# Linear attention and an erf-gated MLP: one-pass products for all units of the second group, and the output product moved ahead of h

## The chip, the cores and the metric

One core of a Trainium2 chip runs the whole kernel. The metric is the device time of the program in microseconds, lower is better. TensorE is called PE in the profile (its weight loads PEld), VectorE DVE, ScalarE ACT, GpSimd POOL and the queue that issues most DMAs SP.

## The reference

```python
# q, k, v: (8, 8, 576, 64), w_in: (512, 2048), w_out: (2048, 512), all float32
kv  = einsum('bhsd,bhse->bhde', k, v)
o   = einsum('bhsd,bhde->bhse', q, kv)
x   = o / sqrt(mean(o * o, axis=-1) + 1e-6) * g_norm      # per head
x   = x.transpose(0, 2, 1, 3).reshape(4608, 512)
h   = x @ w_in                                            # (4608, 2048)
g   = h * erf(log1p(exp(h)))                              # erf of softplus
out = g @ w_out                                           # (4608, 512)
```

## The kernel before

The 4608 tokens are worked in nine groups of 512 columns. Group T holds 512 tokens of batch T; the last group holds the 64 tokens that are left over in each batch. For a group, x lies transposed as xT (four chunks of 128 rows by 512 tokens). The 2048 columns of h are cut into FC = 16 chunks, so a group has 16 units. For each unit the kernel computes h (128 by 512, "hidden"), softplus and erf on ScalarE, the gate `h * s` on VectorE, and the output product of that unit, which adds into four PSUM banks `o_ps`. For groups 0 and 1 (FIRST = 2) a single loop over n = 0 .. 32 goes through the units, n = 16 T + f; for the groups after them a second loop works in batches of four units.

**Two ways to compute a product.** The plain way gives float32 operands to TensorE (L940 for h: four products, which the profile shows as eight instructions; L645 for the output: likewise). The one-pass way (`product`, L589, called by `hidden`) splits both operands. x becomes x_high (rounded, ScalarE, L527), x_low (VectorE, L530) and x_both (VectorE, L533); a weight tile becomes three parts through `w_upper` (one ScalarE operation, L551) and `w_lower` (two VectorE operations, L554 and L557, then a store of the parts to DRAM for the later groups). n_ps takes eight one-pass matmuls (x_high and x_low), m_ps four (x_both). The results are joined by a scaled copy of n_ps on ScalarE (L955) and an add of m_ps on VectorE (L567).

Group 0 uses the plain way throughout. In group 1 the first WHOLE = 2 units (16 and 17) are plain and the others are one-pass. The list `to_cut` says which weight tiles are split in which unit of group 1: in unit f the tile of w_in for unit f + 2, and one of `others` (w_in 0 and 1, then the tiles of w_out); `places_w` adds a third in some units, kept in room that used-up tiles of w_in leave. The parts lie in the pool `w_in_p` with four buffers, which stands where the pool `early` (raw weights, first loads) stood, and is opened when `early` is closed.

**Order.** The order of each engine's instructions is the order in which the program writes them, by hand; engines wait for each other by semaphores. The output product lags: at n, output(n - LAG) with LAG = 5 is computed, in front of it the gate has run at n - 1 (`done = n - LAG + 1`). In group 0 the gate is written ahead of h; in group 1 it is written behind the evacuation:

```python
                nc.scalar.activation(h, n_ps, AF.Copy, scale=SHIFT - 1.0)
                add(h, m_ps)
            if T == FIRST - 1:
                ...
                gates(done)
```

Within one n of group 1 the order before is: pieces of attention at place 3, `w_lower` of tiles cut at n - 1, pieces at place 0 (norm or split), h products, evacuation, gate of unit n - 4, `w_lower` of the third tile, `w_upper` of new tiles, softplus, pieces at place 1 (visit or mean), erf for some units, output(n - 5), and pieces at place 2. The pieces prepare x of the next group: in group 0 that of group 1, in group 1 that of group 2. A "visit" is attention's products on TensorE (L404, L412, L418), a "mean" the sums of squares (L456, L457), followed by Ln, Exp and Square on ScalarE and the norm (L476, L479, L488) with a transpose (L329) on VectorE.

`erf` runs in batches [...] (table loads at L113, L116, L885). `sums` copies the four banks of a finished group out, and `store` sends them to DRAM. Weights arrive as pairs of 32-bit words and are joined to float32 by `w_split` and `w_join` in group 0.

Of the kernel before, what the change touches and what calls it, by code (L numbers as in the profile page):

```python
# [40 lines left out]
FP32R = mybir.dt.float32r  # L41
# [9 lines left out]
BATCH = 4  # L51
LAG = 5
# [1 line left out]


FIRST = 2
WHOLE = 2
SHIFT = 4096.0
SQ = 32
ORDER = """  # L60
# [9 lines left out]
def kernel(  # L70
# [11 lines left out]
    P = 128  # L82
    B, H, S, D = q.shape
    DM, DF = moe_w_in.shape[0], moe_w_in.shape[1] // 2
    J = 4
    G = J * P
    R = S - G
    NP = H // 2
    KC = DM // P
    FC = DF // P  # L90
# [200 lines left out]
    def weights():  # L291

        w_next("split")
        w_next("join")
        w_next("load")
# [229 lines left out]
    def upper(x, high):  # L525

        nc.scalar.activation(high, x, AF.Copy, scale=1.0 + 2.0**-13)  # L527

    def lower_only(x, high, low):
        nc.vector.tensor_tensor(out=low, in0=x, in1=high.bitcast(FP32), op=ALU.subtract)  # L530

    def both_only(high, low, both):
        nc.vector.scalar_tensor_tensor(  # L533
            out=both,
            in0=low.bitcast(FP32),
            scalar=SHIFT,
            in1=high.bitcast(FP32),
            op0=ALU.mult,
            op1=ALU.add,
        )  # L540
# [75 lines left out]
    def w_lower(which, f):  # L616

        t, x, parts = w_new.pop((which, f))
        lower_w(x, *(parts[:, i] for i in range(3)))
        kept = w_kept[which, f] = dram.tile([P, 3, G], FP32, name=f"w_{which}{f}")  # L620
        for i in range(3):
            if t is None:
                nc.sync.dma_start(
                    out=kept[:, i].rearrange("p (c f) -> p c f", c=KC), in_=parts[:, i].bitcast(FP32)
                )
        if t is not None:
            nc.sync.dma_start(out=kept, in_=t.bitcast(FP32))
            if which == "in" and f >= WHOLE:
                w_now[which, f] = [t]

    def hidden(T, f, turns=True):
# [9 lines left out]
    def project(f, g, last):  # L641
        for j in range(J):
            if f == 0:
                o_ps[j] = ps_o.tile([P, DM], FP32, name=f"o_ps{j}", tag=f"o{j}")
            nc.tensor.matmul(  # L645
                o_ps[j],
                lhsT=g[:, j * P : j * P + P],
                rhs=w_out_sb[:, f, :],
                start=(f == 0),
                stop=last,  # L650
            )
# [16 lines left out]
    es = {}  # L668
# [187 lines left out]

    others = [("in", f) for f in range(WHOLE)]
    others += [("out", f) for f in (*range(FC - BATCH, FC), *range(FC - BATCH))]  # L860
    places_w = {3: 0, 5: 1, 6: 0, 8: 1, 9: 2, 10: 0}
    to_cut = {f: [] for f in range(FC)}
    for f in range(FC):
        if f < FC - BATCH:
            to_cut[f] = [others.pop(0), ("in", f + WHOLE)]
        elif f == FC - BATCH:
            to_cut[f] = [("in", FC - 2), ("in", FC - 1)]
        if f in places_w:
            to_cut[f].append((*others.pop(0), places_w[f]))
# [10 lines left out]
    def gates(n):  # L880
        nc.vector.tensor_tensor(out=hs[n], in0=hs[n], in1=ss[n], op=ALU.mult)  # L881

    def erf(units):
        for i in units:
            nc.scalar.activation(ss[i], ss[i], AF.Erf)  # L885

    for n in range(FIRST * FC + 1):
        T, f = divmod(n, FC)
        if n == FC:
            early_room.close()  # L890
            late = ctx.enter_context(tc.tile_pool(name="late", bufs=1))
            x_new = ctx.enter_context(tc.tile_pool(name="x_new", bufs=1))
            acc = ctx.enter_context(tc.tile_pool(name="acc", bufs=1))
            w_in_p = ctx.enter_context(tc.tile_pool(name="w_in_p", bufs=BATCH))
            low = low_room.enter_context(tc.tile_pool(name="low", bufs=1))
            forms = late.tile([P, 3, KC, G], FP32R, name="x_forms0")
            x_forms[FIRST] = [forms[:, i] for i in range(3)]
        if T < FIRST:
            if f == 0:
                steps = pieces_of(T + 1)  # L900

            if due(0 if n == 2 * (BATCH - 1) else 1):
                weights()
            while kept:
                keep_prepared()
            for piece in steps[f][3]:
                piece()
            for key in list(w_new)[:2]:
                w_lower(*key)
            for piece in steps[f][0]:  # L910
                piece()
        while due(0):
            weights()
        done = n - LAG + 1
        if T == 0 and done >= 0:
            gates(done)
        if T == FIRST - 1:
            if f == 0:
                x_high = wide.tile([P, KC, G], FP32R, name="x_high", tag="a")
                x_low = low.tile([P, KC, G], FP32R, name="x_low")  # L920
                for i in range(0, KC, 2):
                    upper(xT[T][:, i : i + 2], x_high[:, i : i + 2])
                for i in range(0, KC, 2):
                    lower_only(xT[T][:, i : i + 2], x_high[:, i : i + 2], x_low[:, i : i + 2])
        if T == FIRST - 1 and f >= WHOLE:
            n_ps, m_ps = hidden(T, f, turns=False)
        elif T < FIRST:

            if n >= AHEAD:
                plain[n] = ps_h.tile([P, G], FP32, name="h_ps", tag="h")  # L930
                blocks = [(n, c) for c in range(KC)]
            elif n == 0:
                for i, (pool, tag) in enumerate(((ps_now[0], "at"), (ps_now[0], "at"), (ps_o, "o0"))):
                    plain[i] = pool.tile([P, G], FP32, name="h_ps", tag=tag)
                blocks = [(i, c) for c in range(2) for i in range(2)]
                blocks += [(2, 0), (2, 1)] + [(i, 2) for i in range(3)] + [(0, KC - 1)]
            else:
                blocks = [(n, KC - 1)]
            for i, c in blocks:
                nc.tensor.matmul(  # L940
                    plain[i],
                    lhsT=w_in_sb[:, i % FC, c],
                    rhs=xT[T][:, c, :],
                    start=(c == 0),
                    stop=(c == KC - 1),
                )
        if T < FIRST:
            if n == whole:
                old_h = acc.tile([P, BATCH, G], FP32, name="h", tag="e")
            h = hs[n] = old_h[:, n - whole] if n >= whole else unit("h_sb")  # L950
            s = ss[n] = unit("s_sb")
            if n in plain:
                nc.scalar.copy(h, plain.pop(n))
            else:
                nc.scalar.activation(h, n_ps, AF.Copy, scale=SHIFT - 1.0)  # L955
                add(h, m_ps)
            if T == FIRST - 1:
                if f == 1:
                    x_both = wide.tile([P, KC, G], FP32R, name="x_both", tag="b")
                    for i in range(0, KC, 2):  # L960
                        both_only(x_high[:, i : i + 2], x_low[:, i : i + 2], x_both[:, i : i + 2])
                    x_forms[T] = x_high, x_low, x_both
                gates(done)
                for key in list(w_new):
                    w_lower(*key)
                for key in to_cut[f]:
                    w_upper(*key)
            if T == FIRST - 1 and f and f % BATCH == 0:
                erf(range(n - BATCH // 2, n))
                softplus_table()  # L970
            nc.scalar.activation(s, h, AF.Softplus)
            for piece in steps[f][1]:
                piece()
            if f % BATCH == BATCH - 1:
                apart = T == FIRST - 1 and f < FC - 1
                erf(range(n - BATCH + 1, n + 1 - (BATCH // 2 if apart else 0)))
                if not apart:
                    softplus_table()
            if T == FIRST - 1:
                load_parts("in", {FC - 3: 2, FC - 2: 1, FC - 1: 1}.get(f, 0))  # L980
        if n >= LAG:
            T2, f2 = divmod(n - LAG, FC)
            last = n - LAG in (FC - 1, whole - 1)
            project(f2, hs[n - LAG], last)
            if last:
                sums(*((acc, "e") if T2 < FIRST - 1 else (wide, "a")))
                if T2 == 0:
                    for j in range(J):
                        store(T2, j, es.pop(j))
        if T < FIRST:  # L990
            for piece in steps[f][2]:
                piece()
            fetch_some(4)
# [49 lines left out]
    for m in range(first_batch, batches + 1):  # L1043
# [10 lines left out]
        def piece():  # L1054
            if todo:
                todo.pop(0)()
# [129 lines left out]
```

## Time and profile before

| what | value |
|---|---|
| median of 3 runs | 907.0 us (906.57 to 907.75) |
| profiled execution | 907.2 us, of which the span is 905.4 us |
| TensorE busy | 897.1 us, 99% |
| VectorE busy | 758.7 us, 84% |
| ScalarE busy | 593.2 us, 66% |
| DMA | 259.89 MB, mean 287 GB/s |
| group 1's products | 125 to 238 us |
| granted TensorE clock | 0.999 |

The page gives for each engine its busy time, and then the chain of work that ended last, followed back from the end. A line of a timeline has the start in us, the length in us, the engine, the line of the kernel, the operation, what it writes and reads, how many instructions are merged, and in brackets how long the engine was idle before it and what ended that. A matmul's end is modelled, and matmuls overlap by pipelining, so the distance between starts says more than the lengths.

### The profile page before, as it was taken

How to read it: one execution, taken by the hardware profiler on the slowest of the kernel's cores; microseconds unless marked ns; L12 is line 12 of the kernel's file. 1: busy time of each engine (PE TensorE's matmuls, PEld its weight loads, DVE VectorE, ACT ScalarE, POOL GpSimd, SP SyncE). 2: the span in 40 equal slices, each digit the busy share in tenths (PEclk: the TensorE clock that was granted, in tenths of full speed). 3: DMA queues.
4: the chain of work that ended last, by engine and by line, in shares of the span. 5: the costliest groups of instructions: out<-in, count | busy, mean ns of one | idle time of the engine just before them, and what ended most of it. 6: DMA issues, size and time to landing. Idle time of an engine off the chain costs nothing.

```text
span 905.4 us, 13399 instructions
## 1 busy us (share of the span) xinstructions
PE 897.1 (99%) x4934; PEld 667.6 (74%) x4934; DVE 758.7 (84%) x1093; ACT 593.2 (66%) x784; POOL 4.7 (1%) x14
## 2 busy tenths in 40 slices
PE   8999999999999999999999999999999999999998
PEld 4444446666688888888888888888888888888886
DVE  5799959997788888888888888888888888887677
ACT  5976677775766666665666666666666766665552
POOL 2000000000000000000000000000000000000000
PEclk9999999999999999999999999999999999999999
DMA  9977308999599988988899879988797788778871
GB/s 290 300 225 222 100 30 289 367 343 354 200 377 375 328 297 262 376 306 300 300 328 364 310 238 327 362 303 305 277 346 274 266 311 311 285 285 314 320 265 48
DMA packets 136930, 259.89 MB, mean 287 GB/s; under 512 B 78817, under 2 KB 87265, under 8 KB 136865
## 3 DMA queue, kind: packets, MB, share of 16 engines
q1 hardware_dynamic: 136128, 258.09, 81.3%
q10 hardware_dynamic: 544, 0.82, 0.3%
q8 instruction: 39, 0.64, 0.3%
q14 instruction: 27, 0.21, 0.1%
q0 software_dynamic: 192, 0.13, 0.0%
HBM read 224.40 MB, written 34.60 MB: 286 GB/s over the span
## 4 chain that ended last, share of the span: by engine, by line
PE 94%; DMA 2%; DVE 2%; ACT 1%; issue 0%; SPq 0%; DVEq 0%
PE n_ps L589 48%; PE m_ps L589 24%; PE o_ps L645 10%; PE h_ps L940 5%; PE at_ps L418 2%; PE at_ps L404 2%; DMA w_out_parts<-w_out 1%; DMA w_raw<-in_moe_w_out_dram 1%; PE at_ps L456 1%; PE at_ps L457 1%; PE warm_ps L792 1%; DVE w_e L267 0%; PE o_ps L712 0%; DVE w_in_sb L274 0%; DVE h L881 0%
## 5 line engine op out<-in xcount | busy, mean ns | idle before, releaser
L589 PE MATMUL n_ps<-w_out_parts,g_forms 128*128 128x512 f32 x928 | 230.5, 390 | 0.1
L589 PE MATMUL n_ps<-x_forms,w_in_parts 128*128 128x512 f32 x896 | 224.3, 392 | 0.0
L589 PEld LDWEIGHTS n_ps<-w_out_parts,g_forms 128*128 128x128 f32 x928 | 172.7, 188 | 36.0 <-DMA w_out_parts<-w_out 0.5
L589 PEld LDWEIGHTS n_ps<-x_forms,w_in_parts 128*128 128x128 f32 x896 | 166.6, 188 | 35.6 <-ACT s_sb L885 0.2
L567 DVE TENSOR_TENSOR h<-m_ps,h 128x512 f32<-128x512 f32 x116 | 78.1, 687 | 63.9 <-PE m_ps L589 61.9
L589 PE MATMUL m_ps<-w_out_parts,g_forms 128*128 128x512 f32 (+1 forms) x468 | 124.2, 388 | 0.0
L589 PE MATMUL m_ps<-x_forms,w_in_parts 128*128 128x512 f32 x448 | 119.7, 389 | 0.0
L1092 ACT ACTIVATE h<-n_ps 128x512 f32<-128x512 f32 x112 | 66.2, 594 | 75.0 <-PE n_ps L589 74.7
L1097 ACT ACTIVATE s<-h 128x512 f32<-128x512 f32 x112 | 68.3, 629 | 70.0 <-DVE h L567 70.0
L645 PE MATMUL o_ps<-w_out_sb,h_sb 128*128 128x512 f32 x224 | 101.5, 596 | 0.2 <-DVE h_sb L881 0.2
L589 PEld LDWEIGHTS m_ps<-w_out_parts,g_forms 128*128 128x128 f32 x468 | 87.4, 188 | 18.4
L589 PEld LDWEIGHTS m_ps<-x_forms,w_in_parts 128*128 128x128 f32 x448 | 84.1, 188 | 17.5
L567 DVE TENSOR_TENSOR e<-m_ps,e 128x512 f32<-128x512 f32 (+1 forms) x117 | 80.3, 687 | 15.4 <-PE m_ps L589 5.6
L645 PEld LDWEIGHTS o_ps<-w_out_sb,h_sb 128*128 128x128 f32 x224 | 41.3, 189 | 45.3 <-issue 43.1
L533 DVE SCALAR_TENSOR_TENSOR g_forms<-g_forms 128x1024 fp32r<-128x1024 f32 x58 | 71.1, 1225 | 2.0
L530 DVE TENSOR_TENSOR g_forms<-h,g_forms 128x1024 fp32r<-128x1024 f32 x58 | 70.5, 1216 | 1.1 <-ACT g_forms L527 1.1
L527 ACT ACTIVATE g_forms<-h 128x1024 fp32r<-128x1024 f32 x58 | 58.4, 1049 | 15.3 <-DVE h L1146 7.9
L562 DVE SCALAR_TENSOR_TENSOR e<-n_ps,e 128x512 f32<-128x512 f32 x88 | 60.2, 684 | 7.3 <-PE n_ps L589 7.3
L940 PE MATMUL h_ps<-xT,w_in_sb 128*128 128x512 f32 x144 | 65.1, 595 | 1.1 <-DVE w_in_sb L274 1.1
L1146 DVE TENSOR_TENSOR h<-h,s 128x1024 f32<-128x1024 f32 x56 | 65.9, 1218 | 0.0
L116 ACT ACT_TABLE_LOAD x44 | 56.5, 1283 | 0.8
L940 PEld LDWEIGHTS h_ps<-xT,w_in_sb 128*128 128x128 f32 x144 | 26.9, 190 | 35.4 <-issue 31.4
(138 smaller groups left out, 999.0 us busy)
## 6 DMA issues: line engine op xcount, KB each, us to landing
w_out_parts<-w_out SPq DMA_DIRECT2D x116, 768.0 KB, 6.8
w_in_parts<-w_in SPq DMA_DIRECT2D x112, 768.0 KB, 6.7
w_in<-w_new SPq DMA_DIRECT2D x16, 768.0 KB, 4.6
k_sb<-in_k_dram SPq DMA_DIRECT2D x32, 288.0 KB, 6.3
v_sb<-in_v_dram SPq DMA_DIRECT2D x31, 288.0 KB, 6.3
w_raw<-in_moe_w_in_dram SPq DMA_DIRECT2D x16, 512.0 KB, 5.6
w_raw<-in_moe_w_out_dram SPq DMA_DIRECT2D x8, 1024.0 KB, 5.1
out_dram<-e SPq DMA_DIRECT2D x32, 256.0 KB, 3.5
```

The costliest lines, as they stand in the source:

```text
L116: nc.scalar.preload_act_table_set("softplus")
L527: nc.scalar.activation(high, x, AF.Copy, scale=1.0 + 2.0**-13)
L530: nc.vector.tensor_tensor(out=low, in0=x, in1=high.bitcast(FP32), op=ALU.subtract)
L533: nc.vector.scalar_tensor_tensor(out=both, in0=low.bitcast(FP32), scalar=SHIFT, in1=high.bitcast(FP32), op0=ALU.mult, op1=ALU.add,)
L562: nc.vector.scalar_tensor_tensor(out=out_, in0=ps, scalar=scale, in1=out_, op0=ALU.mult, op1=ALU.add)
L567: nc.vector.tensor_tensor(out=out_, in0=ps, in1=out_, op=ALU.add)
L589: nc.tensor.matmul(ps[:, cols], lhsT=weights(form, k), rhs=moving(form, k)[:, cols], start=(form == forms[0] and k == 0), stop=(form == fo ...
L645: nc.tensor.matmul(o_ps[j], lhsT=g[:, j * P : j * P + P], rhs=w_out_sb[:, f, :], start=(f == 0), stop=last,)
L940: nc.tensor.matmul(plain[i], lhsT=w_in_sb[:, i % FC, c], rhs=xT[T][:, c, :], start=(c == 0), stop=(c == KC - 1),)
L1092: nc.scalar.activation(h[:, i], n_ps, AF.Copy, scale=SHIFT - 1.0)
L1097: nc.scalar.activation(s[:, i], h[:, i], AF.Softplus)
L1146: nc.vector.tensor_tensor(out=part(h, half), in0=part(h, half), in1=part(s, half), op=ALU.mult)
```

## The change

WHOLE is gone: units 16 and 17 are computed by `hidden` like the others. What they need is made in unit n = 15, the last of group 0. The pool `early` is closed and its successors are opened there (after a loop that joins any weights still left), `w_upper` is called for w_in 0 and 1, and, as `w_lower` follows in the same unit, both tiles are split and stored there; x_high is rounded behind unit 15's softplus and ahead of its erf. x_low and x_both are made at the head of n = 16. `others` loses its first two entries and `places_w` the entries of units 3 and 5 of the group. From n = 16 on, the output product, now the function `output`, is written ahead of the h products of the same n; for n < 16 it stays where it was. The gates stay where they were.

```diff
 FIRST = 2
-WHOLE = 2
...
-            if which == "in" and f >= WHOLE:
+            if which == "in":
                 w_now[which, f] = [t]
...
-    others = [("in", f) for f in range(WHOLE)]
-    others += [("out", f) for f in (*range(FC - BATCH, FC), *range(FC - BATCH))]
-    places_w = {3: 0, 5: 1, 6: 0, 8: 1, 9: 2, 10: 0}
+    others = [("out", f) for f in (*range(FC - BATCH, FC), *range(FC - BATCH))]
+    places_w = {6: 0, 8: 1, 9: 2, 10: 0}
...
-            to_cut[f] = [others.pop(0), ("in", f + WHOLE)]
+            to_cut[f] = [others.pop(0), ("in", f + 2)]
...
+    def output(i):
+        T2, f2 = divmod(i, FC)
+        last = i in (FC - 1, whole - 1)
+        project(f2, hs[i], last)
+        if last:
+            sums(*((acc, "e") if T2 < FIRST - 1 else (wide, "a")))
+            if T2 == 0:
+                for j in range(J):
+                    store(T2, j, es.pop(j))
+
     for n in range(FIRST * FC + 1):
         T, f = divmod(n, FC)
-        if n == FC:
-            early_room.close()
...
         if T < FIRST:
             if f == 0:
                 steps = pieces_of(T + 1)
             if due(0 if n == 2 * (BATCH - 1) else 1):
                 weights()
+            if n == FC - 1:
+                while w_at["join"] < len(w_order):
+                    weights()
+                early_room.close()
...
+                for i in range(2):
+                    w_upper("in", i)
             while kept:
                 keep_prepared()
...
         if T == 0 and done >= 0:
             gates(done)
+        if n == FC:
+            x_low = low.tile([P, KC, G], FP32R, name="x_low")
+            for i in range(0, KC, 2):
+                lower_only(xT[T][:, i : i + 2], x_high[:, i : i + 2], x_low[:, i : i + 2])
+            x_both = wide.tile([P, KC, G], FP32R, name="x_both", tag="b")
+            for i in range(0, KC, 2):
+                both_only(x_high[:, i : i + 2], x_low[:, i : i + 2], x_both[:, i : i + 2])
+            x_forms[T] = x_high, x_low, x_both
+        if n >= FC:
+            output(n - LAG)
         if T == FIRST - 1:
-            if f == 0:
-                x_high = wide.tile([P, KC, G], FP32R, name="x_high", tag="a")
...
-        if T == FIRST - 1 and f >= WHOLE:
             n_ps, m_ps = hidden(T, f, turns=False)
...
             nc.scalar.activation(s, h, AF.Softplus)
             for piece in steps[f][1]:
                 piece()
+            if n == FC - 1:
+                x_high = wide.tile([P, KC, G], FP32R, name="x_high", tag="a")
+                for i in range(0, KC, 2):
+                    upper(xT[1][:, i : i + 2], x_high[:, i : i + 2])
...
-        if n >= LAG:
-            T2, f2 = divmod(n - LAG, FC)
-            last = n - LAG in (FC - 1, whole - 1)
-            project(f2, hs[n - LAG], last)
...
+        if LAG <= n < FC:
+            output(n - LAG)
```

More of the change, by code (lines that the diff above doesn't have):

```diff
@@ L885, in erf @@
             nc.scalar.activation(ss[i], ss[i], AF.Erf)
+    def output(i):
[7 more added lines that the diff above has]
+                    store(T2, j, es.pop(j))
     for n in range(FIRST * FC + 1):
         T, f = divmod(n, FC)
-        if n == FC:
-            early_room.close()
[L891 to L897, printed above, removed]
         if T < FIRST:
@@ L903 @@
                 weights()
+            if n == FC - 1:
+                while w_at["join"] < len(w_order):
+                    weights()
+                early_room.close()
+                late = ctx.enter_context(tc.tile_pool(name="late", bufs=1))
+                x_new = ctx.enter_context(tc.tile_pool(name="x_new", bufs=1))
+                acc = ctx.enter_context(tc.tile_pool(name="acc", bufs=1))
+                w_in_p = ctx.enter_context(tc.tile_pool(name="w_in_p", bufs=BATCH))
+                low = low_room.enter_context(tc.tile_pool(name="low", bufs=1))
+                forms = late.tile([P, 3, KC, G], FP32R, name="x_forms0")
+                x_forms[FIRST] = [forms[:, i] for i in range(3)]
+                for i in range(2):
+                    w_upper("in", i)
             while kept:
@@ L916 @@
             gates(done)
-        if T == FIRST - 1:
-            if f == 0:
-                x_high = wide.tile([P, KC, G], FP32R, name="x_high", tag="a")
[L920 to L924, printed above, removed]
-        if T == FIRST - 1 and f >= WHOLE:
+        if n == FC:
[8 more added lines that the diff above has]
+            output(n - LAG)
+        if T == FIRST - 1:
             n_ps, m_ps = hidden(T, f, turns=False)
@@ L957 @@
             if T == FIRST - 1:
[L958 to L962, printed above, removed]
                 gates(done)
@@ L980 @@
                 load_parts("in", {FC - 3: 2, FC - 2: 1, FC - 1: 1}.get(f, 0))
-        if n >= LAG:
-            T2, f2 = divmod(n - LAG, FC)
-            last = n - LAG in (FC - 1, whole - 1)
-            project(f2, hs[n - LAG], last)
[L985 to L989, printed above, removed]
+        if LAG <= n < FC:
+            output(n - LAG)
         if T < FIRST:
```

## The prediction

> **What bounds the kernel now.** I read the page's busy times and chain, then the table of windows for the second group's stretch, then the timeline by engine there.
>
> ```profile
> PE 897.1 (99%) x4934; PEld 667.6 (74%) x4934; DVE 758.7 (84%) x1093; ACT 593.2 (66%) x784; POOL 4.7 (1%) x14
> ...
> PE 94%; DMA 2%; DVE 2%; ACT 1%; issue 0%; SPq 0%; DVEq 0%
> ```
>
> TensorE is busy for 99% of the span and carries 94% of the chain that ended last: whatever lengthens its queue lengthens the kernel. The second group (units 16 to 31) lies at 125 to 238 us, and inside it TensorE has no hole at all (columns: window, its length, then busy us of PE, PEld, DVE, ACT and POOL):
>
> ```profile
> 135.00:178.00 43.00, 43.00 (x229) 26.31 (x228) 39.14 (x65) 32.51 (x51) 0.00 (x0) 1.00 0.90 324
> ```
>
> The chain in order of time gives the price of a plain h (four products in full fp32, eight instructions) and of an output product: 3.43 us each.
>
> ```profile
> 125.32 3.43 PE h_ps L940 x8
> 128.75 3.43 PE o_ps L645 x8
> 132.18 3.43 PE h_ps L940 x8
> ```
>
> A later unit, on TensorE's timeline, has the one-pass h (n_ps, then m_ps) followed by its output product:
>
> ```profile
> 175.87 1.10 PE L589 MATMUL m_ps<-x_both,w_new 128*128 128x512 f32 x4
> 176.80 3.60 PE L645 MATMUL o_ps<-w_out_sb,h_sb 128*128 128x512 f32 x8
> 179.84 0.79 PE L589 MATMUL n_ps<-x_high,w_new 128*128 128x512 f32 x1
> ...
> 182.11 1.10 PE L589 MATMUL m_ps<-x_both,w_new 128*128 128x512 f32 x4
> 183.04 3.60 PE L645 MATMUL o_ps<-w_out_sb,h_sb 128*128 128x512 f32 x8
> ```
>
> From output to output is 183.04 - 176.80 = 6.24 us; less 3.43, the one-pass h costs 2.81. Now what VectorE does when an h is finished, where it was waiting for it:
>
> ```profile
> 189.55 0.69 DVE L567 TENSOR_TENSOR h_sb<-m_ps,h_sb 128x512 f32<-128x512 f32 x1 [0.67 <-PE m_ps L589]
> 190.16 0.68 DVE L881 TENSOR_TENSOR h_sb<-h_sb,s_sb 128x512 f32<-128x512 f32 x1
> ```
>
> The add of m_ps (unit n), and right behind it the gate (L881) of unit n-4, which the *next* output product reads. Today the whole of hidden(n+1) lies between this gate and its reader, so it costs nothing. Only once does an output product follow without an h between: the last of the group.
>
> ```profile
> 233.65 0.68 DVE L881 TENSOR_TENSOR h_sb<-h_sb,s_sb 128x512 f32<-128x512 f32 x1
> ...
> 234.38 0.30 PEld L645 LDWEIGHTS o_ps<-w_out_sb,h_sb 128*128 128x128 f32 x2 [1.06 <-DVE h_sb L881]
> 234.38 0.70 PE L645 MATMUL o_ps<-w_out_sb,h_sb 128*128 128x512 f32 x1 [0.23 <-DVE h_sb L881]
> ```
>
> There the weight load starts 0.05 us after the gate's end (233.65 + 0.68 = 234.33), and TensorE stands.
>
> [...] No view of this kernel shows a lower clock (1.00 even in the first 10 us, where TensorE idled 1.5 us), so no run here shows a fall.
>
> **The change part by part.**
>
> *Units 16 and 17 in one-pass products.* Removed 2 x 3.43, added 2 x 2.81: -1.24 us, all on TensorE's path. Two more copies with scale and two adds of m_ps (0.60 and 0.69) lie on ScalarE and VectorE beside TensorE's work. The evacuation of both banks has an output product (3.43) over it as before.
>
> *The output product ahead of h, for n >= 16.* The order becomes output(n-5), h(n), output(n-4), h(n+1). Output(n-4) needs gate(n-4), and the code still issues that gate behind the add of unit n, which needs the last product of h(n). So after every h TensorE waits. Take m_ps starting at S (four products). TensorE is free for the next at S + 0.93 (175.87 to 176.80). The add starts at S + 1.20 (188.35 to 189.55), the gate 0.61 later (190.16 - 189.55), it takes 0.68, the load starts 0.05 after, and the unprefetched load costs 0.11 (234.38 to the next h's first product at 237.52 is 3.14, against 179.84 - 176.80 = 3.03). The gap is 1.20 + 0.61 + 0.68 + 0.05 + 0.11 - 0.93 = 1.72 us. It comes after h(16) to h(31), 16 times: 27.5 us.
>
> Part of it is filled. Attention's pieces for group 2 stand between h and the next output: four visits (162.40 to 163.79, 1.39 us) after units 17, 21, 25, 29, and four means (170.08 to 170.55, 0.47) after 18, 22, 26, 30. They ran before too, so 4 x 1.39 + 4 x 0.47 = 7.44 comes off: 20.1 us remain.
>
> VectorE must be at the add on time. A unit now takes 6.24 + 1.72 = 7.96 us. From add to add VectorE needed 8.12 before units 23 and 27 (170.35 to 178.47): 0.15 late each. Before unit 31 it is 8.96 (224.09 to 233.05; the norm waits for ScalarE's root): 1.0 late. Sum 1.3 (0 to 4). The old wait and unprefetched load at 234.38 (0.23 + 0.11) go: -0.3.
>
> *Splits in unit 15.* Two weight splits put two copies (0.52 spacing) on ScalarE, four operations (2.65, spacings at 131.94 to 134.59) on VectorE and two stores of 768 KB on SP. ScalarE reaches them when the last table load of unit 14 ends, at 119.17 + 1.28 = 120.45, and had 1.47 us idle there: free. SP issues nothing from 103.5 to 133.4 and POOL nothing at all, so the stores pass nobody. VectorE is another matter: the diff puts the four operations ahead of this:
>
> ```profile
> 119.19 0.69 DVE L476 SCALAR_TENSOR_TENSOR u<-at_ps,u 128x512 f32<-128x512 f32 x1 [3.61 <-ACT u L470]
> ...
> 121.43 0.78 DVE L329 STREAM_TRANSPOSE qT<-q_sb 128x576 f32<-128x576 f32 x1
> 122.13 0.65 DVE L881 TENSOR_TENSOR h_sb<-h_sb,s_sb 128x512 f32<-128x512 f32 x1
> ```
>
> They start at about 121.1 (first copy's end), so the norm begins at 123.8 rather than 119.2 and gate(11) ends at 123.77 + 2.94 + 0.68 = 127.39 instead of 122.78. It feeds output(11), now the next thing after output(10), whose end is 125.15. TensorE waits until 127.44, plus 0.11: 2.4 us. Nothing in the old trace shows this; bounds are 0 (should the gate come in time) and 4 (should the copies be held too).
>
> *x split.* The two roundings (2.0 us on ScalarE) go ahead of unit 15's erf, the four VectorE operations (4.8) to the head of unit 16. x_high is done at about 127.1 (its second half waits for the norm, 126.0), x_low at 129.8, x_both at 132.1; h(16) starts at 127.55 + 3.4 = 130.9 and wants x_both at 132.8: hidden by output(11), with 0.7 us to spare. The erf of units 12 to 15 ends near 130.6 instead of 126.7; gate(12) asks for it at 134.7: free.
>
> *Rest.* The join loop ahead of the new pools finds nothing left (the last join ends at 115). The third cut of units 19 and 21 is gone from ScalarE (0.52) and VectorE (1.3), both off the path. Sums of group 0 and their four stores come one h earlier, behind the same output(15), with 2.81 us of h over 1.4 us of copies: nothing. At the end h(31) lies behind output(26), leaving output(27) and eight of group 2's products before its sums' banks and gates are wanted; the longest chain I can follow (erf, copies, cut, evacuation of unit 32) has over 3 us left: nothing, 0 to 2.
>
> Sum: -1.2 + 20.1 + 1.3 - 0.3 + 2.4 = **+22.3 us**. The profiled execution took 907.2 (span 905.4 and 1.8 around it), 0.2 above the median of 907.0, so 929.5 against it and **929** against the median. A measurement can tell about 0.2% (1.8 us) from no change.
>
> **The rivals.** *A: the gate is early.* If output(n-4)'s gate ended before h(n) did, the gaps vanish, and so would the stall: 907.0 - 1.2 - 0.3 = 905.5, ahead by 0.17%, with a little luck by more. The mechanism would be slack on VectorE: it waits idle before 189.55. Against it: those 0.67 us are a wait for m_ps itself, and the add stands in front of the gate in one queue. It decides below a gap of 0.2 us: eight units have no piece to fill it, and 8 x 0.2 is the 1.5 us gained. Add and gate alone take 1.29. Chance 3%.
>
> *B: as forecast but without the stall in unit 15 and with lags hidden*: 929 - 2.4 - 1.3 = 925. Some 15%, inside the range.
>
> *C: the gaps slow TensorE's clock.* It would idle 1.72 of 7.96 us, 22%. [...] Against it, [...] a clock of 1.00 at 0 to 10 us in spite of gaps. Chance 4%.
>
> *D: the split does not reach units 16 and 17's products in time*, so that h(16) waits for x_both beyond the 0.7 us: 929 + 3 = 932. Some 10%, inside.
>
> **How the numbers follow.** Forecast with B and D 93%, A 3%, C 4%. The gap at 1.5 or 1.95 instead of 1.72 moves 16 x 0.22 = 3.5 either way; the stall 0 to 4; lags 0 to 4. Low: 929 - 2.4 - 3.5 = 923; high: 929 + 3.5 + 3.5 = 936. Faster by over 0.2%: 1%; within: 2%; slower: 97%.
>
> **What would show it.** In the new profile the output product's weight loads (L645's counterpart) should wait for the gate 16 or 17 times, some 20 to 27 us in all; TensorE busy in the second group should fall to near 85%; output to output should be about 8.0 us with or without a visit between; later stages should keep their lengths. I am wrong if outputs come 6.2 us apart, if the waits name another releaser (x_both, m_ps), or if the clock drops below 1.00.

## The result, and the profile after

| | before | changed |
|---|---|---|
| median, us | 907.35 (906.57 to 907.75) | 930.82 (928.47 to 932.16) |
| ratio to before, 95% interval | | 1.0254 (1.0242 to 1.0267) |
| profiled execution, us (span) | 907.2 (905.4) | 931.17 (929.4) |
| TensorE busy, us | 897.1 | 901.6 |
| granted TensorE clock, mean | 0.999 | 0.995 |

The kernel is 2.5% slower. (907.35 takes in a fourth run of the kernel before; the prediction had three, 907.0.) The page of the changed kernel, busy times and chain by engine:

```profile
PE 901.6 (97%) x4942; PEld 669.8 (72%) x4942; DVE 760.8 (82%) x1095; ACT 593.9 (64%) x784; POOL 4.7 (1%) x14
...
PE 90%; DVE 5%; DMA 2%; ACT 2%; SPq 1%; issue 1%; DVEq 0%; ACTq 0%
```

TensorE's busy time rose by only 4.5 us while the span rose by 24.0: most of the loss is idle time. VectorE's share of the chain went from 2% to 5%. The waits inside the second group (engine and line that waited, for whom, us in total, times, longest), TensorE's rows only:

```profile
PE o_ps L644 <- DVE h_sb L879: 19.6, 17, 2.5
```

There is one kind of wait: the output product waits for the gate, 17 times. The table of windows for the whole stretch (window, length, busy us of PE, PEld, DVE, ACT, POOL, clock, DMA share, GB/s):

```profile
125.00:262.00 137.00, 117.42 (x538) 68.59 (x537) 93.73 (x153) 83.18 (x124) 0.00 (x0) 0.98 0.66 236
262.00:929.00 667.00, 662.74 (x3753) 543.95 (x3751) 566.70 (x786) 421.16 (x540) 0.00 (x0) 1.00 0.85 302
```

TensorE is busy for 86% of the group's stretch and 99% of the rest. Its timeline for the same unit as in the prediction (h of unit 23, then the next output; first an output behind a mean):

```profile
184.37 3.70 PE L644 MATMUL o_ps<-w_out_sb,h_sb 128*128 128x512 f32 x8 [0.98 <-DVE h_sb L879]
192.29 3.70 PE L644 MATMUL o_ps<-w_out_sb,h_sb 128*128 128x512 f32 x8 [1.48 <-DVE h_sb L879]
200.20 3.70 PE L644 MATMUL o_ps<-w_out_sb,h_sb 128*128 128x512 f32 x8 [1.45 <-DVE h_sb L879]
208.10 3.70 PE L644 MATMUL o_ps<-w_out_sb,h_sb 128*128 128x512 f32 x8 [0.16 <-DVE h_sb L879]
```

Outputs now come 7.9 us apart. With nothing between h and output the idle time is 1.45 to 1.48, with a mean 0.98, with a visit 0.16; the distance is the same in all three cases, since the gate, not the piece, ends the gap. (The idle time counts from a matmul's modelled end, the gap in the prediction from when the next could have started, 0.17 earlier, plus 0.11 for the unprefetched load.)

VectorE at units 15 and 16:

```profile
121.07 0.69 DVE L553 SCALAR_TENSOR_TENSOR w_new<-w_new,w_in_sb 128x512 fp32r<-128x512 f32 x1 [5.55 <-ACT w_new L550]
...
123.73 0.68 DVE L475 SCALAR_TENSOR_TENSOR u<-at_ps,u 128x512 f32<-128x512 f32 x1
...
126.67 0.65 DVE L879 TENSOR_TENSOR h_sb<-h_sb,s_sb 128x512 f32<-128x512 f32 x1
```

The weight splits wait 5.55 us for ScalarE's copies, the norm stands behind them, and the gate of unit 11 behind the norm, 4.5 us later than before. TensorE pays for it, and then for something else (outputs 10 and 11, h of unit 16, output 12):

```profile
121.65 3.60 PE L644 MATMUL o_ps<-w_out_sb,h_sb 128*128 128x512 f32 x8
127.37 5.40 PE L644 MATMUL o_ps<-w_out_sb,h_sb 128*128 128x512 f32 x8 [2.13 <-DVE h_sb L879]
132.21 0.80 PE L588 MATMUL n_ps<-x_high,w_new 128*128 128x512 f32 x1
...
134.43 1.09 PE L588 MATMUL m_ps<-x_both,w_new 128*128 128x512 f32 x4
136.97 3.70 PE L644 MATMUL o_ps<-w_out_sb,h_sb 128*128 128x512 f32 x8 [1.45 <-DVE h_sb L879]
140.11 0.80 PE L588 MATMUL n_ps<-x_high,w_new 128*128 128x512 f32 x1
```

The eight instructions of output 12 take 140.11 - 136.97 = 3.14 us from their first start to the next product's start; those of output 11 take 132.21 - 127.37 = 4.84. The windows give the reason (the number behind POOL's is the clock):

```profile
128.00:129.00 1.00, 1.00 (x3) 0.43 (x2) 1.00 (x2) 0.99 (x3) 0.00 (x0) 0.57 0.00 0
129.00:130.00 1.00, 1.00 (x2) 0.33 (x1) 0.97 (x2) 1.00 (x3) 0.00 (x0) 0.50 0.00 0
130.00:131.00 1.00, 1.00 (x2) 0.33 (x1) 1.00 (x2) 0.98 (x3) 0.00 (x0) 0.50 0.00 0
131.00:132.00 1.00, 1.00 (x3) 0.52 (x2) 0.98 (x1) 0.82 (x1) 0.00 (x0) 0.73 0.00 0
```

TensorE was granted half its clock for 3.41 us (0.50 from 128.13 to 131.54), beginning 0.8 us after the hole. I call such a stretch a drop. The same happens behind the last hole, 2.49 us ahead of output 27 (0.50 from 257.84 to 261.25; the output takes from 256.81 to 261.64, 4.83 us). Each costs 1.7 us. One drop lowers the mean clock by 0.5 x 3.4 / 929 = 0.0018, and the half clock in this trace's last 2.55 us (926.84 to 929.39), where TensorE has nothing left to do, takes off 0.5 x 2.55 / 929 = 0.0014 without costing anything. By that measure and their times (an estimate: only the run of 931.17 us was traced) the four runs of the changed kernel had no drop (928.47 us at a mean clock of 1.000), one (930.47 at 0.998) and two each (931.17 at 0.995, 932.16 at 0.996).

### The profile page after: what moved, and what is told of

The parts are those of the page before. It is cut to its first block, busy times and chain, and to the rows that moved or that the text cites. A ratio compares the mean times of both kernels' runs of the same rounds, so it can differ in the third digit from the quotient of the medians.

```text
span 929.4 us, 13404 instructions
## 1 busy us (share of the span) xinstructions
PE 901.6 (97%) x4942; PEld 669.8 (72%) x4942; DVE 760.8 (82%) x1095; ACT 593.9 (64%) x784; POOL 4.7 (1%) x14
## 4 chain that ended last, share of the span: by engine, by line
PE 90%; DVE 5%; DMA 2%; ACT 2%; SPq 1%; issue 1%; DVEq 0%; ACTq 0%
PE n_ps L588 48%; PE m_ps L588 24%; PE o_ps L644 9%; PE h_ps L954 5%; PE at_ps L417 2%; PE at_ps L403 1%; DVE h_sb L879 1%; DMA w_raw<-in_moe_w_in_dram 1%; DVE h_sb L566 1%; SPq L143 1%; PE at_ps L455 1%; PE at_ps L456 1%; DMA w_raw<-in_moe_w_out_dram 1%; ACT L112 0%; DVE qT L328 0%
## 5 line engine op out<-in xcount | busy, mean ns | idle before, releaser
L644 PE MATMUL o_ps<-w_out_sb,h_sb 128*128 128x512 f32 x224 | 106.2, 618 | 19.6 <-DVE h_sb L879 19.6
L954 PE MATMUL h_ps<-xT,w_in_sb 128*128 128x512 f32 x128 | 57.9, 596 | 1.1 <-DVE w_in_sb L273 1.1
L1126 ACT ACTIVATE s<-s 128x1024 f32<-128x1024 f32 x50 | 50.6, 1053 | 0.3
```

The source lines that it names most:

```text
L644: nc.tensor.matmul(o_ps[j], lhsT=g[:, j * P : j * P + P], rhs=w_out_sb[:, f, :], start=(f == 0), stop=last,)
L954: nc.tensor.matmul(plain[i], lhsT=w_in_sb[:, i % FC, c], rhs=xT[T][:, c, :], start=(c == 0), stop=(c == KC - 1),)
```

## The experiments

Theory: in group 1 the gate of unit n - 4 stands on VectorE behind the add of unit n, so an output product placed straight behind h waits for add and gate. Rivals: the one-pass units and their splits cost the time, or the new order costs it for another reason (banks, x_both, parts).

**1. The order alone**, on the kernel before, with units 16 and 17 plain:

```diff
...
+        if n >= FC:
+            output(n - LAG)
         if T == FIRST - 1 and f >= WHOLE:
             n_ps, m_ps = hidden(T, f, turns=False)
...
-        if n >= LAG:
...
+        if LAG <= n < FC:
+            output(n - LAG)
```

(Not shown: the function `output`, as in the change, and the lines that it replaces.)

> The kernel before with only the order changed: the output product ahead of h from unit 16 on; units 16 and 17 stay plain, the splits stay where they were. Theory: 14 waits (behind h of units 18 to 31) of 1.72 us, less 6.05 filled by pieces, 1.3 late adds, about 1.9 behind unit 17 whose gate stands behind x_both, one clock drop 1.7: 907.35 + 22 = 929 us, 926 to 931. Rival (the one-pass units and the splits moved to unit 15 carry much of the loss): under 920 us.

Measured: 928.07 us, ratio 1.0231 (1.0215 to 1.0246), as forecast. TensorE's waits:

```profile
PE o_ps L645 <- DVE h_sb L881: 17.6, 15, 2.5
```

It waits for the gate alone; there is one drop, at the last hole (5.20 us for that output). The four runs show the price of a drop once more: 927.14 and 927.27 us at a mean clock of 0.999, 928.86 and 929.23 at 0.998. The order alone brings nearly the whole loss.

**2. The one-pass units alone**, with the output product behind h throughout:

```diff
-        if n >= FC:
-            output(n - LAG)
...
-        if LAG <= n < FC:
+        if n >= LAG:
             output(n - LAG)
```

> The changed kernel with the output product back behind h in all units; one-pass units and splits stay as changed. Theory: no waits for gates, but h of unit 16 now follows output 10 directly and must wait for x_low and x_both, so it ends near 132.9 instead of 128.0 us, 4.9 late, perhaps with a clock drop (1.7): 907.35 - 1.2 + 4.9 = 911, up to 913 us. Rival (the splits in unit 15 are the main cost): 920 us or more.

Measured: 910.98 us, ratio 1.0042 (1.0026 to 1.0059), as forecast. TensorE's timeline names the price, the x split of unit 16 with no output product over it:

```profile
128.70 0.50 PE L588 MATMUL n_ps<-x_low,w_new 128*128 128x512 f32 x1 [3.03 <-DVE x_low L529]
131.10 0.73 PE L588 MATMUL m_ps<-x_both,w_new 128*128 128x512 f32 x2 [0.30 <-DVE x_both L532]
132.23 0.73 PE L588 MATMUL m_ps<-x_both,w_new 128*128 128x512 f32 x2 [0.40 <-DVE x_both L532]
```

So the output ahead of h is worth something once, in unit 16, and costs in the other units.

**3 and 4. The gate ahead of the add**, at the place it has in group 0; in 4 also unit 15's weight splits behind the gate of unit 11:

```diff
-        if T == 0 and done >= 0:
+        if done >= 0 and T < FIRST:
             gates(done)
...
             if T == FIRST - 1:
-                gates(done)
                 for key in list(w_new):
                     w_lower(*key)
```

```diff
-            for key in list(w_new)[:2]:
+            for key in list(w_new)[:2] if n != FC - 1 else ():
                 w_lower(*key)
...
             gates(done)
+        if n == FC - 1:
+            for key in list(w_new):
+                w_lower(*key)
```

> The changed kernel, but in group 1 the gate of unit n-4 is written ahead of the add of unit n, as in group 0. Theory (TensorE waits for the gate because it stands behind the add): all waits of outputs 12 to 27 go, only the stall of unit 15 (2.1 us) and a clock drop behind it (1.7) stay; 907.35 - 1.2 + 2.3 + 1.7 = 910 us, 909 to 912. Rival (the new order as such costs the time: bank evacuation, x_both or weight parts late): the outputs wait for something else and the time stays above 920 us.

> As the run with the gate ahead of the add, and the weight splits of unit 15 on VectorE are put behind the gate of unit 11. Theory: no wait for a gate is left, so what remains is the saving of the two one-pass units, 907.35 - 1.2 - 0.3 = 905.8 us (905.3 to 906.6). Rival (x_both comes too late for h of unit 16, or the splits' new place makes it late): TensorE waits for x_both or for the weight parts and the time is 908 us or more.

Measured: 925.0 us, ratio 1.0192 (1.0177 to 1.0207), and 922.97 us, ratio 1.0169 (1.0153 to 1.0184). Both forecasts failed: in both the sixteen waits had shrunk to four long ones (in 3 also output 11's, and in each 1.1 us of small ones). VectorE and TensorE in experiment 4, around one of them:

```profile
152.85 0.69 DVE L475 SCALAR_TENSOR_TENSOR u<-at_ps,u 128x512 f32<-128x512 f32 x1 [1.37 <-ACT u L469]
...
155.79 0.65 DVE L879 TENSOR_TENSOR h_sb<-h_sb,s_sb 128x512 f32<-128x512 f32 x1
```

```profile
148.34 3.59 PE L644 MATMUL o_ps<-w_out_sb,h_sb 128*128 128x512 f32 x8
156.50 3.70 PE L644 MATMUL o_ps<-w_out_sb,h_sb 128*128 128x512 f32 x8 [1.74 <-DVE h_sb L879]
...
186.30 3.70 PE L644 MATMUL o_ps<-w_out_sb,h_sb 128*128 128x512 f32 x8 [2.06 <-DVE h_sb L879]
...
215.80 5.32 PE L644 MATMUL o_ps<-w_out_sb,h_sb 128*128 128x512 f32 x8 [2.06 <-DVE h_sb L879]
...
247.56 6.49 PE L644 MATMUL o_ps<-w_out_sb,h_sb 128*128 128x512 f32 x8 [3.06 <-DVE h_sb L879]
```

I had moved the gate ahead of the add, but it now stood behind the norm, which in every fourth unit waits for ScalarE's root (1.37 us of idle ahead of L475). 1.74 + 2.06 + 2.06 + 3.06 = 8.9 us of waiting, and two of the four holes brought a drop (5.32 and 6.49 us instead of 3.70, together 4.4; in experiment 3 the three of 2.06, 2.06 and 3.1 us did, the one of 2.11 ahead of output 11 did not). In unit 16 the gate also stood ahead of x_low and waited 1.58 us for an erf. The theory of the add was not wrong, but too narrow: what counts is everything that stands ahead of the gate.

**5. The gate ahead of norm and add** (in unit 16 behind x_both), weight splits as in 4:

```diff
+            if T == FIRST - 1 and f:
+                gates(n - LAG + 1)
             for piece in steps[f][0]:
                 piece()
...
             x_forms[T] = x_high, x_low, x_both
+            gates(done)
```

> The changed kernel with the gate of unit n-4 behind the weight splits but ahead of the norm and the add (in unit 16 behind x_both), and unit 15's weight splits behind the gate of unit 11. Theory (output waits only for what stands ahead of its gate on VectorE; with the gate ahead of the add alone, four gates stood behind a norm that waits for ScalarE, and one behind an erf): no waits for gates remain, 907.3 - 1.2 - 0.3 = 905.8 us, 905.2 to 907. Rival (output ahead of h needs more than the gate, such as the sums of group 0 or the add of m_ps): some other wait takes over and it stays over 912 us.

Measured: 911.18 us, ratio 1.0043 (1.0029 to 1.0056). Between the theory and the rival: the new order is kept, only the gate and the splits have moved, and 19.6 us of the 23.5 lost are back. Of 19.6 us of waiting for gates 1.0 is left, so the gate was the cause of the gaps; but in part other waits came up that the gaps had covered (TensorE's waits in the group):

```profile
PE o_ps L644 <- DVE e L677: 1.2, 1, 1.2
PE m_ps L588 <- ACT e L675: 1.1, 1, 1.1
PE o_ps L644 <- DVE h_sb L879: 1.0, 2, 0.6
PE n_ps L588 <- DMA w_out_parts<-w_out: 0.9, 1, 0.9
```

The output of unit 16 waits for the sums of group 0 to leave its banks (they stand behind the split of x on VectorE), an h of group 2 for the sums of group 1, which stand behind the group's last erf on ScalarE, and the first result of group 2 for weights whose load was issued late. Sum 4.2 us; against the 905.8 forecast 5.4 are to be explained. The other 1.2 are about what these idle times leave out: as with the gaps above, each of the five waits stands some 0.17 longer and most are followed by a load that costs 0.11 more (estimate: 1.3 us).

**6. The output product ahead of h in unit 16 only**, gates as changed, unit 15's weight splits as in 4:

```diff
-        if n >= FC:
+        if n == FC:
             output(n - LAG)
...
-        if LAG <= n < FC:
+        if n >= LAG and n != FC:
             output(n - LAG)
```

> The changed kernel with the output product ahead of h in unit 16 only and behind h from unit 17 on, gates where they were (behind the add), unit 15's weight splits behind the gate of unit 11. Theory: every gate again has an h in front of its reader, unit 16 keeps the output that covers the x split; 907.3 - 1.2 = 906.0 us, 905.4 to 907. Rival (two h in a row, 16 and 17, wait for their PSUM banks, or x_both is late): 908 us or more.

Measured: 906.33 us (906.05 to 906.76), ratio 0.9990 (0.9982 to 0.9998), as forecast: 0.1% ahead of the kernel before, hardly more than the noise, and 24.5 us ahead of the change. TensorE's only wait left in the group, and its start of the group:

```profile
PE o_ps L644 <- DVE h_sb L879: 0.2, 1, 0.2
```

```profile
121.96 7.03 PE L644 MATMUL o_ps<-w_out_sb,h_sb 128*128 128x512 f32 x16
...
130.71 1.10 PE L588 MATMUL m_ps<-x_both,w_new 128*128 128x512 f32 x4
133.48 1.09 PE L588 MATMUL m_ps<-x_both,w_new 128*128 128x512 f32 x4
```

Outputs 10 and 11 run together (sixteen instructions), h(16) and h(17) follow without a hole. With the gates untouched and all units one-pass, putting the outputs back removes the loss (the splits' move alone is worth 1.3 us, experiment 7): it was the order against the gate, not the products.

**7. Unit 15's weight splits behind the gate of unit 11, alone** (the second diff of 3 and 4):

> The changed kernel with only the weight splits of unit 15 moved behind the gate of unit 11 on VectorE. Theory: the 2.1 us wait of output 11 and, in runs that have one, the clock drop of 1.7 behind it go: 930.8 - 2.1 - (0 to 1.7) = 927.0 to 928.7 us; 16 waits stay. Rival (the wait of output 11 only moves, to x_both of unit 16): 930 us or more.

Measured: 929.49 us, ratio 1.0246 (1.0232 to 1.0260), above the forecast of 927.0 to 928.7. The wait of output 11 is gone (its sixteen instructions with output 10 run as one group), and output 12 starts at 133.41 instead of 136.97 although output 10 started 0.5 later (122.16 against 121.65): 4.1 us, the stall's 2.3 and the drop's 1.7. The medians differ by 1.3, the two profiled runs by 2.6. Two things took the rest. By the mean clock two of the four runs still had two drops (930.63 and 930.38 us at 0.996) and two had one (928.60 and 928.61 at 0.998). And the following units came 7.98 us apart in half of the cases against 7.91, once 8.34 (output 20, behind a gap of 1.80); why is open.

**8. Two unused products in each of the two longest holes:**

```diff
+        if n in (FC, FIRST * FC):
+            idle = ps_h.tile([P, G], FP32, name="idle_ps", tag="h")
+            for i in range(2):
+                src = xT[1][:, i] if n == FC else hs[n - LAG - 1]
+                nc.tensor.matmul(idle, lhsT=src[:, 0:P], rhs=src, start=True, stop=True)
         if n >= FC:
             output(n - LAG)
```

> The changed kernel with two plain products more (1.7 us, into a spare PSUM tile nobody reads) in each of TensorE's two longest holes, ahead of outputs 11 and 27. Theory (the clock drops of 1.7 us behind these two holes come from TensorE standing idle there): the waits stay but the drops go, granted clock 1.000 and about 928.5 us in all runs. Rival (the drops have another cause, or the added products push the outputs back): clock as before, 930.8 us or more.

Measured: 929.76 us (929.63 to 930.96), mean clock 1.000, 1.000, 0.999 and 1.000 in the four runs. TensorE's timeline at the last hole:

```profile
254.57 1.98 PE L941 MATMUL idle_ps<-h_sb 128*128 128x512 f32 x4 [0.24 <-ACT h L974]
256.74 3.70 PE L644 MATMUL o_ps<-w_out_sb,h_sb 128*128 128x512 f32 x8 [0.18 <-DVE h_sb L879]
259.87 2.39 PE L588 MATMUL n_ps<-x_forms,w_in_parts 128*128 128x512 f32 x8
```

The output starts when it did (256.74 against 256.81), but takes 3.13 us to the next product instead of 4.83. That four runs of four had no drop, and only one of four in the changed kernel, speaks for the idle time as the cause of the drops; this one trace does not prove it, since in other traces long holes brought none either (2.11 us in experiment 3, 3.03 in experiment 2). The gain in the median is 1.1 us, not the 2.3 forecast: in this run too part of the units came 7.98 us apart and one 8.35, so that output 27 starts 128.69 us after output 11, against 129.44 - 1.7 = 127.7 in the changed kernel.

## Why the prediction was right

Forecast 929, range 923 to 936; measured 930.8. Its steps against the trace:

- *The gap behind each h, 1.72 us, 16 times.* Right. Ahead of output 12 the wait measures 136.97 - (134.43 + 0.93) = 1.61, and the load that was not prefetched adds 3.14 - 3.03 = 0.11: 1.72. The output products 12 to 27 lie 256.81 - 136.97 = 119.8 us apart; the forecast had 15 x 7.96 and 1.3 for late adds, 120.7. Most of the 0.9 is a cheaper h: its eight products of n_ps took 134.43 - 132.21 = 2.22 us, and 2.27 in the unit that the forecast was made from (182.11 - 179.84). The same work in the old order comes to 15 x 6.24 + 7.44 = 101.0. So gaps and lags cost 18.8, 1.61 ahead of output 12 and 0.11 behind output 27, 20.5 us against 21.4 forecast. Experiments 1 and 6 show from both sides that the order is the cause: the order alone brings the loss, and with the gates untouched the old order takes it away. Experiment 5 shows that the gate is the link: it keeps the new order, moves the gate, and the gaps go. No product passed a waiting output: all 17 waits (19.6 us) end with the output itself, and after output 11 (127.37) the h of unit 16 starts at 132.21.
- *Pieces fill the gaps but do not change the distance.* Right (the four lines of the changed kernel's timeline).
- *Late adds.* Ahead of unit 31 the distance is 256.81 - 247.87 = 8.94 instead of 7.91, 1.0 as forecast; 0 and 0.2 for units 23 and 27 (216.00 to 224.09) against 0.15 each.
- *The stall of output 11, 2.4 us.* Output 10's start plus 3.43 is 125.08, and output 11 starts at 127.37: 2.3, with the load's 0.11 2.4. The chain of causes (copies at 120.4, splits, norm, gate) was as written, to 0.1 us. Experiment 7 removes it.
- *x split hidden by output 11.* Right with the change's timing; experiment 2 shows 3.7 us of waits for x_low and x_both when that cover is gone.
- *The clock.* This was the rival given 4%: the gaps slow TensorE's clock. It was set aside, and in part it came true. The two longest holes, 2.13 and 2.49 us, were each followed by a drop that cost 4.84 - 3.14 = 1.7 us; the other fifteen, 0.16 to 1.64 us, were followed by none, so it was two events and not one behind every gap. They put 3.4 us into the profiled run that the forecast did not have, and one of its own signs of being wrong, a clock below 1.00, came true. The prediction's statement that no run showed a fall was a misreading. The old trace has one in its last 2.3 us, half clock from 903.11, 2.1 us after the last product, and that is where its mean of 0.999 comes from; and the 1.00 of its first 10 us says little, as its clock records begin only at 5.4 us.

Sum for the profiled run: 20.5 + 2.4 + 3.4 - 1.2 - 0.3 = 24.8 (with the forecast's own -1.2 and -0.3) against 24.0 measured; the 0.8 stays open. So the mechanism and the gap were right, and the near hit of the total is in part luck: h a little too dear and a remainder on one side, and the drops that were left out on the other, partly cancelled. What the prediction did not see at all is what experiment 5 brought up. Its rival without gaps counted on 905.5 us, but the new order would still have taken 911.2, with 3.2 us of waits for sums and loads and 1.0 for gates.

## What to carry to other kernels

Ahead of moving a consumer on the bound engine, look at what stands in front of its producer on the producer's own queue: an operation that waits for the same engine's latest product makes a closed loop, and its latency is paid on every turn (here 1.72 us behind each of 16 h). A move that is needed once (here to cover the x split in unit 16) should be made once and not for the whole loop. And a fix has to be traced again, since a gap can cover several other waits: moving the gate ahead of the add alone took away twelve of the sixteen waits, and left four behind the next thing that stood in front of it.

## What the runs showed of the hardware

- Idle holes of TensorE of 2.06 to 3.06 us were followed by a half clock in some cases and by the full clock in others. Both drops in the changed kernel's trace last 3.41 us. The holes, each with the start of the product behind it and the mean granted clock of a window there:

| run | hole, us | product behind it at, us | window, us | clock in it |
|---|---|---|---|---|
| changed kernel | 2.13 | 127.37 | 128.13 to 131.54 | 0.50 |
| changed kernel | 2.49 | 256.81 | 257.84 to 261.25 | 0.50 |
| experiment 3 | 2.11 | 128.24 | 128 to 132 | 1.00 |
| experiment 3 | 2.06 | 188.18 | 186 to 192 | 0.76 |
| experiment 4 | 2.06 | 186.30 | 186 to 190 | 1.00 |
| experiment 4 | 2.06 | 215.80 | 215 to 221 | 0.72 |
| experiment 4 | 3.06 | 247.56 | 247 to 254 | 0.56 |
| experiment 2 | 3.03 | 128.70 | 129 to 133 | 1.00 |

A window longer than the drop mixes half and full clock. The two holes of 2.06 us in experiment 4 went both ways, and the one of 3.03 us in experiment 2 brought no drop, so the length of a hole alone does not decide; what else does was not shown.
- In experiment 2 three runs had a mean clock of 0.997 and the profiled one 1.000, yet all four took 910.84 to 911.14 us. Where in the three the clock was lower, and why it cost nothing, was not shown.
- One-pass matmuls came 0.227 us apart in some units and 0.236 in others (unit 17 of the changed kernel at 140.74 to 142.10, unit 23 of the kernel before at 174.22 to 175.63), up to 0.07 us for the eight of an h. The runs do not show what sets it.
